# Moving row sums and norm matmuls behind the value matmuls, and summing a layer's last tile in halves

## The chip, the core and the metric

One core of a Trainium2 chip runs the whole program. The metric is the device time of one launch in microseconds (us), the median of several runs. Engines are named as the profile names them: PE (TensorE matmul) with its weight loads PEld, DVE (VectorE), ACT (ScalarE), POOL (GpSimd), SP (SyncE, which here only issues DMAs).

## The reference

The input x has 2048 rows of 1024 values. Two layers run one after the other, each an attention block and a spectral block:

```python
x = x + attention(layernorm(x))   # 32 heads of 32 columns, 2048 queries by 2048 keys, then @ wo
x = x + spectral(layernorm(x))    # rfft2, times complex weights, irfft2
...
scores = einsum("bhqd,bhkd->bhqk", q, k) * 32 ** -0.5
p = softmax(scores); o = einsum("bhqk,bhkd->bhqd", p, v); return o @ wo
```

## The kernel before, in words

**The main loop of attention.** The 32 heads are taken in 8 groups g of 4 heads, the queries in 4 chunks c of 512, the keys in 16 tiles kt of 128. One pass of the loop, here called a step, is one (g, c, kt). In each step `S` writes scores into two tiles of the PSUM pool `psS` (three tiles of two banks each), and ACT takes the exponential of both into two `p` tiles (line 552; the `p` pool has eight tiles, so four steps). K and Q are split into two fp16 parts, so `S` is 12 matmuls on 32 rows each. In every even step `PV` multiplies the `p` tiles of the two steps before by V (line 558): four fp32 matmuls per step, each on 32 columns of the array, which the trace shows as 16 PE instructions for the two steps.

**Row sums.** The softmax's denominators are summed on DVE: `add` adds each `p` tile into an accumulator `acc` of two halves (line 569 for the first two steps of a chunk together, which overwrites `acc`; line 571 after that). There is one `acc` only. When a chunk is through, `fin` multiplies `acc` by ones on PE (`z`, line 577, four fp32 matmuls on 32 columns, eight PE instructions in the trace, into a tile of `psS`), and DVE transposes, inverts, transposes back and scales the chunk's output (lines 578 to 584). `out` then makes two fp16 parts of it, the high one on ACT (line 590), the low one on POOL (line 591), and a DMA stores them.

**Work between the steps.** In odd steps a generator `fill` feeds PE with the projections of the groups to come, paced by `slots`: 8 or so matmuls at a time of `qk_chunk` (K or Q, line 328, 24 matmuls into a PSUM tile `x`) or of `v_tiles` (line 372). Tile `x` is a pool of one. At the end of a `qk_chunk`, `split` reads it twice: ACT writes the high fp16 part (line 167), DVE the low one (line 168), and only then can the next projection start. POOL squares the high part (`sq`, line 332). After the last of four chunks of a K or a Q the phase is put into `left_norms`, and `norms` turns the squares into norms: four bf16 matmuls on 32 columns (line 345) into a tile of `psS`, a maximum on DVE (line 347), and after a Q a bias by way of POOL (`partition_all_reduce`, lines 353 to 358). Group 7 has no projections left; there the slots carry the products with `wo` (`wo_part`, and `wo_rest` for tiles that are ready).

**Order.** In the main loop PE and ACT keep the order in which the source issues their work (`manual_schedule`). The queues of DVE, POOL and SP are ordered by a planner, which works ahead of the run and fixes each queue once.

**A layer's end.** The last four row tiles t = 0 to 3 wait for the last chunk's output. `first(t, ds)` does the products with `wo` for the groups ds of 0 to 6, `last(t)` the one for group 7, by `wo_last`: DVE adds the residual `xres` over all 1024 columns (line 460), takes `bn_stats` of both halves (line 462), a DMA stores the tile, DVE folds it (lines 146, 147), POOL works out scale and bias in eight small instructions (`scale_bias`, lines 119 to 124, 489, 490), ACT and DVE apply them (lines 685, 686). `xres` has a pool of two tiles (`wqk`), so tile t needs tile t-2 to be stored and folded first. `fold_rests` does the same for the twelve tiles before. The spectral block's first transposes (line 762) need all sixteen tiles. In this part only PE keeps the source's order. At the end of the program `combine_flags` gathers checks over all partitions (`partition_all_reduce`, line 1108, on POOL).

The lines of the main loop that are changed, in short:

```python
if kt % 2 == 0:
    for w in pend: PV(*w)          # the two steps before
    late, pend = pend, []
for w in late[:1]:
    add(*w)                        # kt 14 of the last chunk at kt 0, kt 15 at kt 1
    if w[2] == NKT - 1: fin(*w[:2]); done = [w[:2]]
late = late[1:]
if kt == 5 and done: out(*done.pop())
```

and `slots` runs `while left_norms: norms()` ahead of each odd step's projection matmuls.

Of the kernel before, what the change touches and what calls it, by code (L numbers as in the profile page):

```python
# [6 lines left out]
F32 = mybir.dt.float32  # L7
# [4 lines left out]
AF = mybir.ActivationFunctionType  # L12
ALU = mybir.AluOpType
# [88 lines left out]
SW = 2.0 ** 8  # L102
SQ = 2.0 ** 5
SO = 2.0 ** 5
# [23 lines left out]
def ln_stats(nc, sm, cst, st, mv):  # L128

    nc.vector.bn_aggr(mv, st)  # L130
    return ln_scale(nc, sm, cst, mv, nc.vector)
# [9 lines left out]
def fold(nc, x, out, a, eng=None):  # L141

    xv = x.rearrange("p (a u g q) -> p g a u q", a=8, g=2, q=8)[:, :, a]
    ov = out.rearrange("p (u g a q) -> p g a u q", g=2, a=8, q=8)[:, :, a]
    eng = eng or nc.gpsimd
    eng.tensor_tensor(ov[:, 0], xv[:, 0], xv[:, 1], op=ALU.add)
    eng.tensor_tensor(ov[:, 1], xv[:, 0], xv[:, 1], op=ALU.subtract)
# [23 lines left out]
def run(g):  # L171
    for _ in g:
        pass
# [93 lines left out]
def attention(nc, tc, layer, ap, xin, yd, wts, wo, cst, dram, flags):  # L267
# [6 lines left out]
    sq, on, on2, sm = ap.sq, ap.on, ap.on2, ap.sm  # L274
    psS = psum("at_psS", 3, space=PSUM)
# [13 lines left out]
    V, K, Q, bias, nrm, mx = {}, {}, {}, {}, {}, {}  # L289
# [47 lines left out]
    left_norms = []  # L337

    def norms():
        kind, g = ph = left_norms.pop(0)  # L340
        if g not in mx:
            mx[g] = sm.tile([128, 2], F32, name="mqk")
        ps = psS.tile([128, 2, 512], F32, name="s")
        for c in range(4):
            nc.tensor.matmul(ps[32 * c:32 * c + 32, 0], cst["bones"], nrm[ph][:, c], start=True, stop=True)
        i = 0 if kind == "k" else 1
        nc.vector.reduce_max(mx[g][:, i:i + 1], ps[:, 0], axis=AX.X)
        if kind == "q":
            mkbias(g)
# [75 lines left out]
    def wo_mm(p, c, t, n, ds, start=True, stop=True):  # L425

        for d in ds:
            oh, ol = ((olast[c][:, i] if d == 7 else osb[c][:, i, d])[:, t * 128:t * 128 + 128] for i in range(2))
            wh, wl = (wo_t[i][d // 4][:, d % 4, n * 512:n * 512 + 512] for i in range(2))
            for i, (a, b) in enumerate(((oh, wh), (oh, wl), (ol, wh))):  # L430
                nc.tensor.matmul(p, a, b, start=start and d == ds[0] and i == 0, stop=stop and d == ds[-1] and i == 2)  # L431
                yield

    def xres(c, t):
        x = wqp.tile([128, 1024], F32, name="xres", tag="wqk")
        r0 = c * 512 + t * 128
        nc.sync.dma_start(x, xin[r0:r0 + 128, :])
        return x
# [80 lines left out]
    for c in range(NCH):  # L519
        t = 4 * c + 4  # L520
# [33 lines left out]
    def PV(g, c, kt):  # L554
        if kt == 0:
            O[g, c] = psO.tile([128, 512], F32, name="o")
        for h in range(4):
            nc.tensor.matmul(O[g, c][32 * h:32 * h + 32], V[g][:, kt, 32 * h:32 * h + 32], P[g, c, kt, h // 2][:, h % 2],  # L558
                             start=kt == 0, stop=kt == NKT - 1)
        if kt == NKT - 1:  # L560
            o = ap.oc.tile([128, 512], F32, name="oc")
            nc.scalar.copy(o, O[g, c])
            O[g, c] = o
# [9 lines left out]
    def fin(g, c):  # L573
        zt = on.tile([128, 16, 32], F32, name="zt")
        z = psS.tile([128, 2, 512], F32, name="s")[:, 0]
        for h in range(4):
            nc.tensor.matmul(z[32 * h:32 * h + 32], cst["ones"], acc[h // 2][:, h % 2], start=True, stop=True)  # L577
        nc.vector.transpose(zt.rearrange("p a b -> p (a b)"), z)
        rc = sm.tile([128, 16], F32, name="rc")
        nc.vector.reciprocal(rc, zt[:, :, 0])  # L580
        nc.vector.tensor_max(flags["r"], flags["r"], rc)
        r = on.tile([128, 512], F32, name="zt")
        nc.vector.transpose(r.rearrange("p (a b) -> p a b", b=32), rc.unsqueeze(2).broadcast_to([128, 16, 32]))
        nc.vector.scalar_tensor_tensor(r, O[g, c], SO, r, op0=ALU.mult, op1=ALU.mult)
        O[g, c] = r
# [8 lines left out]
        else:  # L594
            olast[c] = t

    pend, done, late = [], [], []
    fill, lwo, wof = filler(), load_wo(), wo_parts()
    left, parts, rests = 16, 20, list(range(12))

    def slots(f, sums, n, steps):

        while sums:
            k = max(1, int(n / sums + 0.5))
            m = -(-steps // k)
            for i in range(0, steps, m):
                while left_norms:
                    norms()
                for _ in range(min(m, steps - i)):
                    next(f, None)  # L610
                n -= 1
                yield sums - (i + m >= steps)
            sums -= 1

    with tc.manual_schedule(engines={mybir.EngineType.PE, mybir.EngineType.Activation}):
        for g in range(NG):
            todo = sum(sums(ph) for ph in beside.get(g, []))
            sl = slots(fill, todo, 22 if g == NG - 2 else 32, 24)
            wsl = slots(wof, 4, 10, 21)
            for u in range(NCH * NKT):  # L620
                c, kt = divmod(u, NKT)
                S(g, c, kt)
                if kt % 2 == 0:
                    for w in pend:
                        PV(*w)
                    late = pend
                    pend = []
                for w in late[:1]:
                    add(*w)
                    if w[2] == NKT - 1:  # L630
                        fin(*w[:2])
                        done = [w[:2]]
                late = late[1:]
                if kt == 5 and done:
                    out(*done.pop())
                pend.append((g, c, kt))
                if kt % 2 == 0:
                    continue
                if todo:
                    todo = next(sl)  # L640
                elif g == NG - 2:
                    if left:
                        run(lwo)
                        left = 0
                    if next(wsl, None) is not None and u == NCH * NKT - 1:
                        run(wsl)
                elif g == NG - 1:
                    t = rests[0] if rests else 16
                    if (t // 4 < c - 1 or t // 4 == c - 1 and kt >= 7) and (kt % 4 == 3 or not parts):
                        wo_rest(rests.pop(0))  # L650
                    elif parts:
                        parts -= 1
                        for _ in range(21):
                            next(wof)
                if g == NG - 2 and todo < 4:
                    for _ in range(2):
                        if left > (8 if todo == 3 else 0):
                            next(lwo, None)
                            left -= 1
        for w in pend:  # L660
            PV(*w)
        for w in late + pend:
            add(*w)
        run(wof)
        for t in rests:
            wo_rest(t)
    with tc.manual_schedule(engines={mybir.EngineType.PE}):
        ps, xs, folds = [], [], fold_rests()

        def first(t, ds):  # L670
            if ds[0] == 0:
                ps.append(psS.tile([128, 2, 512], F32, name="s"))
                xs.append(xres(3, t))
            for n in range(2):
                run(wo_mm(ps[t][:, n], 3, t, n, ds, start=ds[0] == 0, stop=False))

        def last(t):
            o = ap.x[:, 12 + t]
            st = wo_last(3, t, ps[t], xs[t], xs[t], False)
            mv = sm.tile([128, 2], F32, name="mv")  # L680
            nc.vector.bn_aggr(mv, st)
            r, b = scale_bias(mv, 1, 2.0)
            fold(nc, xs[t], o, slice(0, 8), nc.vector)
            ov = o.rearrange("p (u g q) -> p g u q", g=2, q=64)
            nc.scalar.activation(ov[:, 0], ov[:, 0], AF.Identity, bias=b, scale=r)
            nc.vector.tensor_scalar(ov[:, 1], ov[:, 1], r, None, op0=ALU.mult)

        def some(n):
            for _ in range(n):
                next(folds, None)  # L690
        first(0, range(7))
        fin(NG - 1, NCH - 1)
        out(NG - 1, NCH - 1, nc.vector)
        some(6)
        first(1, range(7))
        last(0)
        some(4)
        first(2, range(7))
        last(1)
        run(folds)  # L700
        first(3, range(4))
        last(2)
        first(3, range(4, 7))
        last(3)
    psum.close()
    small.close()

# [491 lines left out]
```

## Time and profile before

| | us |
|---|---|
| median of 3 runs | 3951.18 (3951.08 to 3956.0) |
| the profiled execution | 3952.66, span 3950.8 |
| PE busy | 3770.9 (95%) |
| DVE busy | 3225.5 (82%) |
| ACT busy | 2893.9 (73%) |
| POOL busy | 643.4 (16%) |
| granted TensorE clock | 0.985 |

The span is what lies between the first and the last instruction; some 2 us of the execution lie around it. The main loop of layer 0 runs from about 128 to 1655 us of the span, that of layer 1 from about 2107 to 3614; the rest is preparation, the layers' ends and the spectral blocks. A row of the timeline gives start, length, engine, line, what it writes and reads, how many instructions were merged, and in brackets the idle time before it and what ended it.

### The profile page before, as it was taken

The numbers are of one execution on the slowest core, as the hardware profiler recorded it, in microseconds if no ns is written. First come the engines' busy times: TensorE is split into PE (matmuls) and PEld (weight loads), VectorE is DVE, ScalarE is ACT, GpSimd is POOL, SyncE is SP. The second block draws the span as 40 slices with busy tenths as digits, with TensorE's granted clock in tenths as the row PEclk, the third lists the DMA queues.
The fourth block names the chain that finished last, engine by engine and source line by source line (L and its number), as shares of the span: only waits on it lengthen the run. The fifth ranks groups of instructions, "written<-read, shape, count | busy, mean of one in ns | idle before, by whom it ended". The sixth has DMA issues, their size and how long they took to land.

```text
span 3950.8 us, 80100 instructions
## 1 busy us (share of the span) xinstructions
PE 3770.9 (95%) x33204; PEld 1671.8 (42%) x33204; DVE 3225.5 (82%) x3845; ACT 2893.9 (73%) x3565; POOL 643.4 (16%) x591
## 2 busy tenths in 40 slices
PE   7999999999999999989989999999999999999898
PEld 5322432342243233378854334333422432333787
DVE  6699888989998978866765998899899888788456
ACT  4587887888788766658745888888888887665585
POOL 1011011101110200014321220122021111000143
PEclk9999999999999999999999999999999999999999
DMA  3000000000000211143120000000000002122323
GB/s 116 14 15 19 12 12 17 17 14 19 12 23 12 89 52 68 54 177 108 55 86 12 15 23 12 12 17 24 8 17 17 17 12 89 57 73 83 120 94 102
DMA packets 97559, 177.31 MB, mean 45 GB/s; under 512 B 7200, under 2 KB 52896, under 8 KB 96160
## 3 DMA queue, kind: packets, MB, share of 16 engines
q1 hardware_dynamic: 97040, 172.03, 12.7%
q8 instruction: 262, 4.29, 0.4%
q14 instruction: 113, 0.93, 0.1%
q10 hardware_dynamic: 144, 0.07, 0.0%
HBM read 123.83 MB, written 48.23 MB: 44 GB/s over the span
## 4 chain that ended last, share of the span: by engine, by line
PE 76%; DVE 9%; issue 7%; ACT 4%; POOL 3%; DMA 1%; SPq 0%; DVEq 0%; ACTq 0%; POOLq 0%
PE o L558 21%; PE s L548 17%; PE x L328 13%; PE x L372 8%; PE x L431 6%; DVE R L571 2%; ACT p L552 2%; PE ps L833 2%; PE ps L771 2%; PE s L577 1%; PE o L372 1%; PE ps L762 1%; PE ps L948 1%; PE o L328 1%; PE ps L902 1%
## 5 line engine op out<-in xcount | busy, mean ns | idle before, releaser
L552 ACT ACTIVATE p<-s,bias 128x1024 f32<-128x1024 f32 x2048 | 2168.3, 1111 | 585.0 <-PE s L548 573.8
L571 DVE TENSOR_TENSOR R<-R,p 128x1024 f32<-128x1024 f32 x1792 | 2145.8, 1250 | 142.2 <-ACT p L552 138.1
L558 PE MATMUL o<-p,R 128*32 128x512 f32 x8192 | 985.0, 598 | 0.0
L328 PE MATMUL x<-big,wqk 128*128 128x512 f16 x2880 | 686.6, 384 | 22.7 <-DVE R L168 8.2
L548 PEld LDWEIGHTS <-R 32*128 32x128 f16 x12288 | 231.1, 92 | 781.1 <-issue 664.8
L328 PEld LDWEIGHTS <-wqk 128*128 128x128 f16 x3072 | 277.6, 98 | 460.7 <-issue 169.4
L548 PE MATMUL s<-R 32*128 32x512 f16 x6144 | 431.9, 379 | 19.0 <-ACT p L552 15.5
L548 PE MATMUL s<-Q,R 32*128 32x512 f16 x6144 | 432.0, 378 | 11.9 <-ACT p L552 10.6
L558 PEld LDWEIGHTS o<-p,R 128*32 128x32 f32 x8192 | 213.7, 109 | 523.5 <-issue 522.9
L591 POOL TENSOR_TENSOR ohl<-zt,ohl 128x512 f16<-128x512 f32 x62 | 180.0, 2903 | 1473.4 <-ACT ohl L590 1473.4
L372 PEld LDWEIGHTS <-big 128*128 128x128 f16 x3072 | 293.3, 99 | 117.2 <-issue 69.8
L372 PE MATMUL x<-wv,big 128*128 128x256 f16 x2688 | 323.5, 277 | 12.5 <-DVE R L168 6.0
L569 DVE SCALAR_TENSOR_TENSOR R<-p 128x1024 f32<-128x1024 f32 x128 | 153.8, 1203 | 197.5 <-ACT p L552 197.1
L332 POOL TENSOR_TENSOR sq<-R 128x512 bf16<-128x512 f16 x96 | 142.4, 1483 | 703.0 <-ACT R L167 702.5
L431 PE MATMUL x<-big 128*128 128x512 f16 x1008 | 228.0, 380 | 0.0
L431 PEld LDWEIGHTS <-big 128*128 128x128 f16 x1344 | 126.8, 98 | 177.9 <-issue 35.8
L881 DVE TENSOR_TENSOR H<-G,H 128x512 f16<-128x512 f32 (+1 forms) x68 | 46.8, 688 | 106.1 <-ACT H L880 105.9
L833 PE MATMUL ps<-cbi,H 128*128 128x256 f16 (+1 forms) x792 | 99.1, 273 | 6.2 <-ACT H L880 4.3
L826 ACT COPY U<-ps 64x256 f32<-64x256 f32 (+1 forms) x272 | 97.0, 357 | 7.9 <-PE ps L833 2.7
L826 ACT COPY B<-ps 64x256 f32<-64x256 f32 (+1 forms) x272 | 97.0, 356 | 6.7 <-PE ps L833 2.4
L332 POOL TENSOR_TENSOR sq<-Q 128x512 bf16<-128x512 f16 x32 | 45.1, 1409 | 321.3 <-ACT Q L167 321.3
L833 PE MATMUL ps<-cb,big 128*128 128x256 f16 x780 | 96.3, 273 | 0.0
(418 smaller groups left out, 3145.0 us busy)
## 6 DMA issues: line engine op xcount, KB each, us to landing
wst<-in_wp SPq DMA_DIRECT2D x96, 256.0 KB, 3.0
R<-y SPq DMA_DIRECT2D x32, 512.0 KB, 5.2
w<-in_w SPq DMA_DIRECT2D x60, 256.0 KB, 2.6
od<-ohl SPq DMA_DIRECT2D x56, 256.0 KB, 2.4
big<-od SPq DMA_DIRECT2D x16, 896.0 KB, 7.1
y<-R SPq DMA_DIRECT2D x20, 512.0 KB, 2.6
R<-in_x SPq DMA_DIRECT2D x16, 512.0 KB, 6.6
wst<-in_wo SPq DMA_DIRECT2D x32, 256.0 KB, 3.0
```

The lines of the kernel that those rows point to most:

```text
L328: nc.tensor.matmul(ps, a, b, start=d == 0 and i == 0, stop=d == 7 and i == 2)
L332: nc.gpsimd.tensor_tensor(nrm[ph][:, c], t[:, 0], t[:, 0], op=ALU.mult)
L372: nc.tensor.matmul(ps[:, j], l, r, start=d == 0 and i == 0, stop=d == 7 and i == 2)
L431: nc.tensor.matmul(p, a, b, start=start and d == ds[0] and i == 0, stop=stop and d == ds[-1] and i == 2)
L548: nc.tensor.matmul(s[h // 2][:, h % 2], K[g][r, a, kt * 128:kt * 128 + 128], Q[g][r, b, c * 512:c * 512 + 512], start=i == 0, stop=i == 2)
L552: nc.scalar.activation(p, s[hf], AF.Exp, bias=bias[g], scale=SCALE / (SQ * SQ))
L558: nc.tensor.matmul(O[g, c][32 * h:32 * h + 32], V[g][:, kt, 32 * h:32 * h + 32], P[g, c, kt, h // 2][:, h % 2], start=kt == 0, stop=kt == ...
L569: nc.vector.scalar_tensor_tensor(acc[hf], P[g, c, 0, hf], 1e-34, p, op0=ALU.add, op1=ALU.add)
L571: nc.vector.tensor_add(acc[hf], acc[hf], p)
L591: eng.tensor_tensor(t[:, 1], r, t[:, 0], op=ALU.subtract)
L826: nc.scalar.copy(ov[64 * r:64 * r + 64, a0:a0 + m, x], tl[64 * x:64 * x + 64, :m, r])
L833: nc.tensor.matmul(out, l, r, start=k == 0, stop=k == len(mm_) - 1)
```

## The change

1. In the main loop `fin` moves from step 1 of the next chunk, right behind the scores, to step 2, behind the eight value matmuls that step issues. `add` for the last key tile stays at step 1 and only notes the chunk in `ends`.
2. `norms` leaves `slots` and stands behind the value matmuls of every even step.
3. At a layer's end POOL, too, keeps the source's order.
4. The products for tile 2 start before `last(0)` (three groups), and tile 3 isn't prepared ahead: a new function `whole(3)` does all its products at the very end, in two halves of 512 columns; while PE works on the second, DVE adds the residual of the first, takes its statistics, stores it and folds it. Scale and bias are worked out on DVE but for one power on POOL.

```diff
-    pend, done, late = [], [], []
+    pend, ends, done, late = [], [], [], []
...
-                while left_norms:
-                    norms()
                 for _ in range(min(m, steps - i)):
                     next(f, None)
...
                 if kt % 2 == 0:
                     for w in pend:
                         PV(*w)
+                    if ends and kt == 2:
+                        fin(*ends[0])
+                        done = [ends.pop()]
+                    while left_norms:
+                        norms()
                     late = pend
                     pend = []
                 for w in late[:1]:
                     add(*w)
                     if w[2] == NKT - 1:
-                        fin(*w[:2])
-                        done = [w[:2]]
+                        ends = [w[:2]]
...
-    with tc.manual_schedule(engines={mybir.EngineType.PE}):
+    with tc.manual_schedule(engines={mybir.EngineType.PE, mybir.EngineType.Pool}):
...
+        def whole(t):
+
+            p, x, o = psS.tile([128, 2, 512], F32, name="s"), xres(3, t), ap.x[:, 12 + t]
+            st = sm.tile([128, 2, 6], F32, name="st")
+            r0 = 3 * 512 + t * 128
+            for n in range(2):
+                sl = slice(n * 512, n * 512 + 512)
+                run(wo_mm(p[:, n], 3, t, n, range(8)))
+                nc.vector.scalar_tensor_tensor(x[:, sl], p[:, n], 1.0 / (SO * SW), x[:, sl], op0=ALU.mult, op1=ALU.add)
+                nc.vector.bn_stats(st[:, n], x[:, sl])
+                nc.sync.dma_start(yd[r0:r0 + 128, sl], x[:, sl])
+                fold(nc, x, o, slice(4 * n, 4 * n + 4), nc.vector)
+            mv = sm.tile([128, 2], F32, name="mv")
+            r = ln_stats(nc, sm, cst, st, mv)
+            b = sm.tile([128, 1], F32, name="b1")
+            nc.vector.scalar_tensor_tensor(b, mv[:, 0:1], -2.0, r, op0=ALU.mult, op1=ALU.mult)
+            ov = o.rearrange("p (u g q) -> p g u q", g=2, q=64)
+            nc.scalar.activation(ov[:, 0], ov[:, 0], AF.Identity, bias=b, scale=r)
+            nc.vector.tensor_scalar(ov[:, 1], ov[:, 1], r, None, op0=ALU.mult)
+
         first(0, range(7))
         fin(NG - 1, NCH - 1)
         out(NG - 1, NCH - 1, nc.vector)
         some(6)
         first(1, range(7))
+        first(2, range(3))
         last(0)
         some(4)
-        first(2, range(7))
+        first(2, range(3, 7))
         last(1)
         run(folds)
-        first(3, range(4))
         last(2)
-        first(3, range(4, 7))
-        last(3)
+        whole(3)
```

## The prediction

> **What bounds the kernel now.** I read the page first, then the timeline at the start of a chunk, the busy time by windows, the views of single lines (who waits for whom), and the timeline of the layers' ends.
>
> ```profile
> PE 3770.9 (95%) x33204; PEld 1671.8 (42%) x33204; DVE 3225.5 (82%) x3845; ACT 2893.9 (73%) x3565; POOL 643.4 (16%) x591
> L552 ACT ACTIVATE p<-s,bias 128x1024 f32<-128x1024 f32 x2048 | 2168.3, 1111 | 585.0 <-PE s L548 573.8
> L571 DVE TENSOR_TENSOR R<-R,p 128x1024 f32<-128x1024 f32 x1792 | 2145.8, 1250 | 142.2 <-ACT p L552 138.1
> ```
>
> PE leads: ACT idles 574 us for scores. But DVE isn't far behind, and this change touches just its place. The chunk that starts at 2514.60 shows the pattern:
>
> ```profile
> 2514.60 0.83 PE L548 MATMUL s<-R 32*128 32x512 f16 x12
> 2515.35 1.92 PE L558 MATMUL o<-p,R 128*32 128x512 f32 x16
> 2517.21 0.82 PE L548 MATMUL s<-R 32*128 32x512 f16 x12
> 2517.97 1.06 PE L577 MATMUL s<-R,ones 128*32 128x512 f32 x8
> 2518.07 2.12 ACT L552 ACTIVATE p<-s,bias 128x1024 f32<-128x1024 f32 x2
> 2518.96 1.90 PE L328 MATMUL x<-big,wqk 128*128 128x512 f16 x8
> 2519.22 1.23 DVE L569 SCALAR_TENSOR_TENSOR R<-p 128x1024 f32<-128x1024 f32 x1 [2.12 <-ACT p L552]
> 2520.80 0.83 PE L548 MATMUL s<-R 32*128 32x512 f16 x12
> 2523.41 0.82 PE L548 MATMUL s<-R 32*128 32x512 f16 x12
> 2524.38 5.76 DVE L571 TENSOR_TENSOR R<-R,p 128x1024 f32<-128x1024 f32 x5
> 2526.00 0.82 PE L548 MATMUL s<-R 32*128 32x512 f16 x12
> ...
> 2514.60:2559.90 45.30, 44.27 (x405) 13.30 (x407) 42.52 (x42) 36.71 (x38) 9.26 (x4) 1.00 0.02 8
> ```
>
> Steps start at 2514.60, 2517.21, 2520.80, 2523.41, 2526.00. A plain step is 2.60 of PE; step 1 with the row sums is 3.59. DVE adds at 5.76 / 5 = 1.15 per half, 2.30 per step. The last row (windows: PE, PEld, DVE, ACT, POOL busy) leaves DVE 45.30 - 42.52 = 2.78 us idle in the chunk, and 2.12 of these are the wait ahead of line 569. There is hardly any slack elsewhere.
>
> **The change, part by part.**
>
> *Fewer changes of kind on PE.* Sixteen value matmuls take 2517.21 - 2515.35 = 1.86, the eight of the row sum, alone between scores and projection, 2518.96 - 2517.97 = 0.99. Eight more of the same kind therefore cost 0.87, and 0.12 is the price of standing alone. The row sums join the value matmuls 62 times (31 per layer): -7.4. The norms do 28 times (14 per layer); no row shows their bf16 passes behind fp32 ones, so 0 to 0.12 each, and I take 0.12, as the shape on the array is the same: -3.4. Together -11.
>
> *Waits at the row sums.* The waits of the row sums for the last adds go, as DVE has over 4 us more (first row; the others serve below):
>
> ```profile
>   DVE R L571: 6.1, 7
> ...
>   POOL sq L332: 7.0, 5
> ...
>   DVE R L168: 8.2, 8
>   DVE Q L168: 6.3, 3
> ...
>   PE s L548: 4.6, 7
> ```
>
> (idle time of line 577 ended by the adds; of the norm matmuls by POOL; of the projections by DVE's split, two rows; of scores held by the norms' maximum.) -6.
>
> *The accumulator is free later.* There is one `acc`, and line 569 overwrites it, so it waits for the row sum to have read it. Now it starts 2519.22 - 2517.21 = 2.0 after step 1 began, held by ACT alone. Then: step 1 without sums 2.60, scores and value matmuls 0.75 + 1.74, the sum's first half 0.44, and some 0.2 until DVE knows: 5.7. DVE starts each chunk 3.7 us later, 62 times, with nothing to put into the pause but a split (0.6). This doesn't lengthen the chunk at once: `p` holds four steps, and up to about 5 us of lateness at a chunk's end cost nothing, as the next pause absorbs them. But DVE is late throughout. Line 569 starts 3.1 after step 2; from it to the first line 571 lie 5.16 now, some 4.6 if the split goes into the pause; so the adds of step 2 end 3.1 + 4.6 + 2.3 = 10.0 after that step began, where exponentials (0.86 + 2.12) and one add (1.2) would allow 4.2: late by 5.8. PE gives back 0.30 per step, and 0.87 more at step 2, which the sum makes longer: 5.8 - 5 x 0.30 - 0.87 = 3.4 left at step 7. A POOL operation that gets in between costs DVE more: two adds take 3.56 then, 2.35 without.
>
> ```profile
> 2710.26 9.17 DVE L571 TENSOR_TENSOR R<-R,p 128x1024 f32<-128x1024 f32 x8
> 2719.94 3.56 DVE L571 TENSOR_TENSOR R<-R,p 128x1024 f32<-128x1024 f32 x2
> 2724.03 2.35 DVE L571 TENSOR_TENSOR R<-R,p 128x1024 f32<-128x1024 f32 x2
> ...
> 2712.37 8.07 POOL L591 TENSOR_TENSOR ohl<-zt,ohl 128x512 f16<-128x512 f32 x1 [9.16 <-ACT ohl L590]
> ...
>   L591 POOL TENSOR_TENSOR ohl<-zt,ohl x62: 1162/1831/9315, 193.0 to 3583.7; 128x512 f16<-128x512 f32 x62
> ...
> 2722.47 0.38 PE L345 MATMUL s<-sq,bones 128*32 128x512 bf16 x1 [2.16 <-POOL sq L332]
> ```
>
> So about 4.6 late at step 7. What is behind DVE's queue there? The split that frees tile `x` for the next projection. Layer 0 shows its price, where DVE is late by its own extra work:
>
> ```profile
> 606.24 7.74 DVE L571 TENSOR_TENSOR R<-R,p 128x1024 f32<-128x1024 f32 x6
> 606.53 0.83 PE L548 MATMUL s<-R 32*128 32x512 f16 x12
> 611.73 0.82 PE L548 MATMUL s<-R 32*128 32x512 f16 x12
> 613.90 0.68 DVE L168 SCALAR_TENSOR_TENSOR Q<-x,Q 128x512 f16<-128x512 f32 x1
> 614.64 4.21 PE L328 MATMUL x<-big,wqk 128*128 128x512 f16 x12 [2.08 <-DVE Q L168]
> ```
>
> Step 7 starts at 606.53; its adds end at 613.98, late by 3.2; the split stands behind them in the queue, and the projection of step 9, due at 611.73 + 0.76, waits 2.1. The rule from this row: wait = lateness - 1.1. At 4.6 that is 3.5 per chunk if the queue keeps this order; each half add that the planner puts behind the split takes off 1.15. In the source the split stands before the adds of its own step, and the planner, too, sees the pause; yet the row shows a queue that doesn't follow what really is late. Between 0 (four halves overtaken) and 3.5 (none) I take 1.6, one or two of them. Chunks with K or Q projections: all four of groups 0, 2, 4, three of group 6, the first two of groups 1, 3, 5: 21 per layer, 42. 42 x 1.6 = +67; the waits that stand there now and are part of it (8.2 + 6.3 + 4.6 = 19) come off: +48. V projections free `x` by ACT alone, and group 7 has DVE time to spare: 0 there.
>
> *Norms and POOL.* The norm in the second chunk of groups 0 to 6 (14 times) follows the last square by less: it stands one set of scores earlier (0.76). The square queues behind `out`'s low half, which takes 1.8 us mostly but 8.07 where eight adds follow without a gap. DVE that never pauses makes this the rule. Now these waits are 7.0 in all; then 0 to 3 each, and I take 1.0, nearer to today's rows: 14 - 7 = +7. ACT's copy for `out` at step 5 isn't late: the row sum's DVE work ends some 8 us after step 2, step 5's exponentials later.
>
> In a sentence that the sum doesn't use: the Trainium skill, "SBUF — State Buffer", section "SBUF: two separate sides", says that a VectorE instruction with two SBUF inputs and a GpSimd one share a port pair as an exclusive lock, held for the whole instruction. Taken literally GpSimd would wait for one add at most (1.2 + 1.8 = 3.0 us); the row's 8.07 over eight adds speaks against so early a turn, and by the rule this term would be -7 and the total 3961.
>
> *The layers' ends.*
>
> ```profile
> 1679.78 0.61 PE L431 MATMUL s<-big,ohl 128*128 128x512 f16 x2 [2.59 <-ACT ohl L590]
> 1680.82 1.89 PE L431 MATMUL s<-big,ohl 128*128 128x512 f16 x4 [0.43 <-DVE ohl L591]
> 1704.04 1.46 PE L431 MATMUL s<-big,ohl 128*128 128x512 f16 x6
> 1715.72 2.01 PE L762 MATMUL ps<-ident,R 128*128 128x128 f32 x8 [10.23 <-ACT R L685]
> ...
> 1708.53 1.23 DVE L460 SCALAR_TENSOR_TENSOR xres<-s,xres 128x1024 f32<-128x1024 f32 x1 [2.00 <-DMA xres<-in_x]
> ...
> 3681.03 2.01 PE L762 MATMUL ps<-ident,R 128*128 128x128 f32 x8 [16.26 <-ACT R L685]
> ...
> 3658.60 0.40 POOL L1108 PARTITION_ALL_REDUCE fa<-f  x1 [6.90 <-issue]
> 3667.13 0.25 POOL L119 TENSOR_SCALAR v<-mv 128x1 f32<-128x1 f32 x1 [8.13 <-issue]
> ```
>
> Tile 2's first groups fill the waits of 2.59 + 0.43. From line 460 to the transposes lie 7.2 us; in halves, with 0.6 each, and one POOL step instead of eight, about 4.5. But `xres` of tile 3 comes by a DMA that follows tile 1's store; it ends the wait today. So between 0 and -7 for layer 0; I take -4. Layer 1 idles 6.0 longer, since the planner put the checks' all-reduce among the tiles (6.90 + 8.13 of POOL time); with POOL in source order it comes later, where the spectral block's first stage leaves POOL idle. -4 - 6 = -10, at worst +5, if its wait then holds DVE. SP's queue gets one store more per layer: 0, hidden behind the constants' loads. Together -14.
>
> **The sum.** -11 - 6 + 48 + 7 - 14 = +24. The profiled execution is 3952.7 (span 3950.8 and 1.9 around it), 1.5 above the median 3951.2; so 3977 for a like execution, 3975 as the median.
>
> **Rivals.**
>
> *Faster: the planner re-sorts DVE's queue.* It sees the pause before the row sum, sets splits and maxima ahead of the late adds, and PE never waits. Then -11 - 6 - 19 - 7 - 14 = -57, 3894; with a few waits left, 3906. It decides below (11 + 6 + 19 - 7 + 14) / 42 = 1.0 us of wait per chunk. For it: the source order; against it: the layer-0 rows.
>
> *Much slower: the queue stays as it is.* 2.8 per chunk instead of 1.6, norms at 1.5: +24 + 50 + 7 = +81, 4032; with 3.5, 4062.
>
> *The all-reduce stays among the tiles* although POOL keeps source order, because it lies outside the ordered part: layer 1 gains 4, not 10: 3981. This goes with any other case.
>
> **How the numbers follow.** About 8 us (0.2%) is what a measurement tells from no change. Queue re-sorted, 3894 to 3943: 0.36. Gains and waits even out, within 8: 0.12. Forecast, 3959 to 4010: 0.32 (that is its own range). Much slower, to 4062: 0.20. Range 3903 to 4040, which leaves out some 0.07 below and 0.11 above. Faster 0.36, same 0.12, slower 0.52.
>
> **What would show it.** In the profile after: step 1 shorter by 0.99 and step 2 longer by 0.87; line 569's idle time ended by PE line 577 and not by ACT, some 5 us each; line 328 waiting for DVE line 168 by 50 to 80 us in all (14.5 now); `out` on POOL with a median well above 1.83; line 345 waiting more for POOL; line 762 after 6 to 8 us of idle time in both layers, the all-reduce behind it. Wrong, if line 328's wait stays near 15: then the queue was re-sorted.

## The result, and the profile after

The changed kernel takes 4178.5 us (median of 4 runs, 4173.8 to 4186.1); the kernel before, on the same chip, 3953.6 (3951.1 to 3960.1). The ratio is 1.0569 (95% interval 1.0556 to 1.0582): 5.7% slower. The forecast was 3975, the range 3903 to 4040; the direction came out, which the forecast had given a chance of 0.52, and the size did not. The profiled execution took 4186.1 with a span of 4184.3.

First the page of the changed kernel (per engine: busy time, share of the span, instructions; per group: busy time, mean ns | idle time before it and what ended most of it):

```profile
PE 3826.3 (91%) x33204; PEld 1698.1 (41%) x33204; DVE 3242.1 (77%) x3863; ACT 2895.1 (69%) x3565; POOL 540.7 (13%) x577
L328 PE MATMUL x<-big,wqk 128*128 128x512 f16 x2880 | 734.3, 403 | 157.4 <-DVE R L168 112.3
L569 DVE SCALAR_TENSOR_TENSOR R<-p 128x1024 f32<-128x1024 f32 x128 | 153.9, 1204 | 285.2 <-PE s L577 249.1
```

The row of line 328 in the kernel before:

```profile
L328 PE MATMUL x<-big,wqk 128*128 128x512 f16 x2880 | 686.6, 384 | 22.7 <-DVE R L168 8.2
```

The number of PE instructions is as before, yet PE is busy 55 us longer (3826.3 against 3770.9), and its share of the span falls. Line 569 is now held by the row sums, line 328 by the split. The waits of the changed kernel (who waited for whom: us, times, longest) complete this:

```profile
DVE R L569 <- PE s L577: 249.1, 62, 8.8
PE x L328 <- DVE R L168: 112.3, 29, 4.8
PE x L328 <- DVE Q L168: 36.8, 7, 6.7
PE x L372 <- DVE R L168: 32.5, 6, 5.9
```

Projections wait 112.3 + 36.8 + 32.5 = 181.6 us for the split, 42 times. Where the span grew can be read from the timelines' starts (us between the first score matmul, the last row sum, and the spectral block's first transpose of each layer; "PE idle" is the sum of its matmuls' idle times in the two main loops):

| | main loop, layer 0 | layer 1 | PE idle in both | end, layer 0 | layer 1 |
|---|---|---|---|---|---|
| before | 1538.9 | 1519.0 | 68.5 | 48.8 | 54.8 |
| after | 1644.9 | 1633.3 | 233.1 | 56.1 | 60.9 |

So the main loops cost +220.3, of which 164.6 are idle time of PE and the other 55.7 slower work; the ends cost +13.4; the rest of the program is unchanged (-0.2).

One chunk shows both parts of the main loop's loss. It is the third chunk of group 2 in layer 1, in the timeline of the changed kernel, PE and DVE:

```profile
2716.28 0.83 PE L548 MATMUL s<-R 32*128 32x512 f16 x12
2717.03 2.76 PE L328 MATMUL x<-big,wqk 128*128 128x512 f16 x12
...
2722.23 1.04 PE L577 MATMUL s<-R,ones 128*32 128x512 f32 x8
2723.30 1.22 DVE L569 SCALAR_TENSOR_TENSOR R<-p 128x1024 f32<-128x1024 f32 x1 [2.15 <-PE s L577]
...
2729.83 1.29 DVE L168 SCALAR_TENSOR_TENSOR wqk<-wst,wqk 128x512 f16<-128x512 f32 x2
2731.03 13.25 DVE L571 TENSOR_TENSOR R<-R,p 128x1024 f32<-128x1024 f32 x10
2733.61 0.83 PE L548 MATMUL s<-R 32*128 32x512 f16 x12
...
2744.21 0.68 DVE L168 SCALAR_TENSOR_TENSOR Q<-x,Q 128x512 f16<-128x512 f32 x1
2744.93 4.84 PE L328 MATMUL x<-big,wqk 128*128 128x512 f16 x12 [5.30 <-DVE Q L168]
```

Step 1 starts at 2716.28 and line 569 at 2723.30, 7.0 later; it was 2.0 before. (The third chunk of each group from 0 to 6 has so long a step 1; in the others that follow a row sum it is 6.0 to 6.5, and in group 7 it is 9.0.) Ten half adds (13.25 us) then stand in DVE's queue ahead of the split of line 168. Step 7 starts at 2733.61, its adds end at 2744.28. The projection of step 9 waits 5.30 us for the split. And then its 12 matmuls take 4.84 us, where the same 12 take 2.76 in the second row. The windows of the same timeline (length, then PE, PEld, DVE, ACT, POOL busy, then the granted clock PEclk) say why:

```profile
2716.28:2719.73 3.45, 3.45 (x28) 1.31 (x25) 0.00 (x0) 2.96 (x4) 0.00 (x0) 1.00 0.02 5
2738.81:2749.71 10.90, 5.60 (x28) 1.87 (x25) 10.61 (x10) 2.49 (x3) 0.00 (x0) 0.69 0.00 0
```

In the step without a wait the granted clock is 1.00, in the stretch of the wait and the projection behind it 0.69 (0.56 over the projection alone). The Trainium skill, "TensorE: Matmul & The Clock Gate", section "What's actually happening", says that the array falls to half its clock after an idle window of about 3.4 us and needs about as long of work to come back. The rows agree in kind: 12 matmuls at half the clock would take twice 2.76, 5.5 us as an estimate from the row, and 4.84 were measured. But here shorter waits were enough at times. In the kernel before, 12 projections took 4.21 at a granted clock of 0.63 behind a wait of 2.08 (a row of the prediction), and full speed behind one of 2.07:

```profile
985.25 2.75 PE L328 MATMUL x<-big,wqk 128*128 128x512 f16 x12 [2.07 <-DVE Q L168]
```

The ends of the layers, in the timeline (layer 0, then, behind the dots, layer 1):

```profile
1815.83 0.69 DVE L701 SCALAR_TENSOR_TENSOR xres<-s,xres 128x512 f32<-128x512 f32 x1 [3.00 <-DMA xres<-in_x]
1816.57 6.75 PE L431 MATMUL s<-big 128*128 128x512 f16 x21 [15.18 <-DVE xres L701]
1824.01 0.69 DVE L701 SCALAR_TENSOR_TENSOR xres<-s,xres 128x512 f32<-128x512 f32 x1 [4.61 <-PE s L431]
1829.11 2.01 PE L783 MATMUL ps<-ident,R 128*128 128x128 f32 x8 [5.14 <-ACT R L710]
...
3874.16 0.40 POOL L1129 PARTITION_ALL_REDUCE fa<-f  x1 [19.03 <-DVE f L1125]
3886.31 0.25 POOL L119 TENSOR_SCALAR v<-mv 128x1 f32<-128x1 f32 x1 [11.75 <-issue]
3903.13 6.25 PE L431 MATMUL s<-big 128*128 128x512 f16 x21 [20.45 <-DVE xres L701]
```

The transposes wait only 5.1 us now, in both layers, as they were meant to. But the matmuls of the second half wait 15.2 and 20.5 us until DVE has read the first half, and DVE waits for the load of the residual. Behind that wait 21 matmuls take 6.75 and 6.25 us, where 21 of the same line take 4.70 earlier in the same end (at 1796.05). The all-reduce still stands among the tiles.

### The profile page after: what moved, and what is told of

Read it like the earlier page. It is cut to its first block, busy times and chain, and to the rows that moved or that the text cites. A ratio compares the mean times of both kernels' runs of the same rounds, so it can differ in the third digit from the quotient of the medians.

```text
span 4184.3 us, 79879 instructions
## 1 busy us (share of the span) xinstructions
PE 3826.3 (91%) x33204; PEld 1698.1 (41%) x33204; DVE 3242.1 (77%) x3863; ACT 2895.1 (69%) x3565; POOL 540.7 (13%) x577
## 4 chain that ended last, share of the span: by engine, by line
PE 67%; DVE 15%; issue 11%; ACT 2%; DMA 2%; POOL 2%; SPq 0%; DVEq 0%; POOLq 0%; ACTq 0%
PE o L558 18%; PE s L548 14%; PE x L328 13%; PE x L372 7%; DVE R L571 5%; PE x L431 5%; DVE R L569 2%; PE ps L792 1%; PE ps L854 1%; PE s L577 1%; ACT p L552 1%; PE o L372 1%; PE ps L783 1%; PE ps L969 1%; PE o L328 1%
## 5 line engine op out<-in xcount | busy, mean ns | idle before, releaser
L571 DVE TENSOR_TENSOR R<-R,p 128x1024 f32<-128x1024 f32 x1792 | 2181.3, 1267 | 123.3 <-ACT p L552 122.7
L328 PE MATMUL x<-big,wqk 128*128 128x512 f16 x2880 | 734.3, 403 | 157.4 <-DVE R L168 112.3
L328 PEld LDWEIGHTS <-wqk 128*128 128x128 f16 x3072 | 289.5, 101 | 614.2 <-issue 345.3
L569 DVE SCALAR_TENSOR_TENSOR R<-p 128x1024 f32<-128x1024 f32 x128 | 153.9, 1204 | 285.2 <-PE s L577 249.1
L372 PE MATMUL x<-wv,big 128*128 128x256 f16 x2688 | 329.7, 280 | 38.9 <-DVE R L168 32.5
L591 POOL TENSOR_TENSOR ohl<-zt,ohl 128x512 f16<-128x512 f32 x62 | 85.0, 1371 | 1533.6 <-ACT ohl L590 1533.6
L168 DVE SCALAR_TENSOR_TENSOR R<-x,R 128x512 f16<-128x512 f32 x88 | 60.1, 683 | 80.3 <-ACT R L167 80.3
L431 PE MATMUL s<-big 128*128 128x512 f16 x336 | 77.8, 392 | 35.6 <-DVE xres L701 35.6
```

The costliest lines, as they stand in the source:

```text
L328: nc.tensor.matmul(ps, a, b, start=d == 0 and i == 0, stop=d == 7 and i == 2)
L372: nc.tensor.matmul(ps[:, j], l, r, start=d == 0 and i == 0, stop=d == 7 and i == 2)
L569: nc.vector.scalar_tensor_tensor(acc[hf], P[g, c, 0, hf], 1e-34, p, op0=ALU.add, op1=ALU.add)
L571: nc.vector.tensor_add(acc[hf], acc[hf], p)
L591: eng.tensor_tensor(t[:, 1], r, t[:, 0], op=ALU.subtract)
```

## The experiments

Theory A: the accumulator comes free late; the planner leaves the split behind the half adds, which then are late; PE waits, and runs at a reduced clock after the wait. Rivals: the norms behind the value matmuls, POOL's new order, or DVE having no time left whatever the order.

### One part of the change at a time

`e1_fin_only` is the kernel before with this edit alone:

```diff
                     for w in pend: PV(*w)
+                    if ends and kt == 2:
+                        fin(*ends[0]); done = [ends.pop()]
...
                     if w[2] == NKT - 1:
-                        fin(*w[:2]); done = [w[:2]]
+                        ends = [w[:2]]
```

> The kernel before with one part of the change: the row sums move to step 2 behind the value matmuls; norms and layers' ends stay. Theory A (the accumulator comes free late, DVE is late through the chunk, the split stands behind its adds, and PE waits and then runs slowly): this part is the whole loss of the main loop, +220 us by the two traces (106 in layer 0, 114 in layer 1), the ends as before: 4174, between 4160 and 4190. Theory B (the norms behind the value matmuls share in the loss, since POOL's squares come late): at least 50 less, below 4125. Theory C (the ends with POOL in source order hurt beyond their 13 us): the main loop still +220, so the same 4174.

Measured: 4174.8, ratio 1.0556 (1.0538 to 1.0574). From its page:

```profile
L328 PE MATMUL x<-big,wqk 128*128 128x512 f16 x2880 | 730.5, 402 | 158.1 <-DVE R L168 113.3
```

The row is that of the changed kernel within 4 us, and line 569 idles 243.0 us for the row sums (249.1 there); the main loops take 1639.5 and 1632.4. This one edit alone lengthens the main loops by 214.0 of the changed kernel's 220.3: it is the loss of the main loops but for 6 us.

`e2_ends_only` is the kernel before with the new layers' ends (`whole`, the order of the products, POOL in source order).

> The kernel before with the layers' ends alone changed (the order of the products, the last tile in halves, POOL in source order). Theory A: only what the traces show between the last row sum and the first spectral transpose, +7.3 and +6.1: 3967, between 3961 and 3973. Theory C (POOL's order reaches back into the main loop through the planner): above 3985. My prediction's figure for this part was -14: 3940.

Measured: 3966.0, ratio 1.0023 (1.0014 to 1.0033). Main loops 1541.0 and 1519.2, ends 56.0 and 57.3. POOL's order doesn't reach back into the main loop.

`e3_fin_back` is the changed kernel with `fin` again in step 1 right behind `add`:

```diff
-                    if ends and kt == 2:
-                        fin(*ends[0])
-                        done = [ends.pop()]
...
-                        ends = [w[:2]]
+                        fin(*w[:2])
+                        done = [w[:2]]
```

> The changed kernel with the row sums put back to step 1; norms stay behind the value matmuls and the ends stay new. Theory A: main loop as before, less 3 to 6 for fewer changes of kind at the norms, ends +13: 3962, between 3956 and 3970. Theory B: the norms cost by themselves, above 3985.

Measured: 3970.8, ratio 1.0034 (1.0020 to 1.0048), just above what was expected. Against `e2_ends_only`, from which it differs by the norms alone, the main loops are -0.2 and +5.3: no gain by the norms can be seen.

### What turns a late accumulator into a wait

`e5_dve_order` is the changed kernel, row sums late as they are, with one more engine in source order:

```diff
-    with tc.manual_schedule(engines={mybir.EngineType.PE, mybir.EngineType.Activation}):
+    with tc.manual_schedule(engines={mybir.EngineType.PE, mybir.EngineType.Activation, mybir.EngineType.DVE}):
```

> The changed kernel, but DVE too keeps the source's order in the main loop, so that each split stands ahead of the adds of its own and the next step, whose exponentials come later. The accumulator is as late as in the changed kernel. Theory A1 (the wait is a matter of queue order: four half adds stand ahead of the split): waits of line 328 for line 168 fall from 112 to under 20 us, the slow projections behind them go, main loop -200: 3965 with the ends' +13, between 3945 and 3990. Theory A2 (DVE has no time left: it idles 4.6 us per chunk where it had 2.8 us in all, and PE must wait for it somewhere whatever the order): (4.6 - 2.8) x 42 = 76 at least remain: above 4040. If source order holds DVE behind the row sum's transposes or behind a split that waits for a load, line 552 or 571 would show it, and the time could be above 4178.

Measured: 3948.1, ratio 0.9980 (0.9970 to 0.9990): 230 us faster than the changed kernel, and a little faster than the kernel before in spite of the slower ends. Its page:

```profile
L328 PE MATMUL x<-big,wqk 128*128 128x512 f16 x2880 | 684.3, 383 | 14.8 <-DVE Q L168 7.3
```

and its timeline in group 2, layer 1, at the start of the first chunk:

```profile
2467.39 0.83 PE L548 MATMUL s<-R 32*128 32x512 f16 x12
2469.98 0.83 PE L548 MATMUL s<-R 32*128 32x512 f16 x12
2473.45 0.83 PE L548 MATMUL s<-R 32*128 32x512 f16 x12
...
2476.13 2.35 DVE L569 SCALAR_TENSOR_TENSOR R<-p 128x1024 f32<-128x1024 f32 x2
2478.40 4.62 DVE L571 TENSOR_TENSOR R<-R,p 128x1024 f32<-128x1024 f32 x4
2482.94 0.68 DVE L168 SCALAR_TENSOR_TENSOR R<-x,R 128x512 f16<-128x512 f32 x1
2483.86 0.39 PE L548 MATMUL s<-R 32*128 32x512 f16 x4
```

Line 569 starts 2476.13 - 2467.39 = 8.7 us after step 1 began, later than in the same chunk of the changed kernel (2623.33 - 2617.11 = 6.2). But only four half adds of line 571 stand between it and the split, which is done about when step 7 begins. DVE has time enough; the rival that it has none falls. The order decides. Main loops: 1526.8 and 1506.6, 24.5 less than before. Source order changes all of DVE's queue, so that this run shows the order as the cause, not the split's place alone.

`e8_before_order` has the same edit on the kernel before.

> The kernel before with one edit: DVE keeps the source's order in the main loop. With the row sums at step 2, source order made the main loop 24.5 us shorter than that of the kernel before (1526.8 + 1506.6 against 1538.9 + 1519.0). This run parts the two causes. If source order does it alone (waits for splits and maxima, 19 us in the kernel before): 3935, between 3930 and 3941. If fewer changes of kind and the row sums' waits for adds do it (11 + 6 of my sum): only some 7 us here, 3950, between 3944 and 3957. If at step 1 source order makes DVE wait for the row sums' transposes: above 3957.

Measured: 4087.3, ratio 1.0335 (1.0315 to 1.0355): none of the two expected causes, but the case that was named last and without a size. In the waits (who waited for whom: us, times, longest):

```profile
DVE zt L578 <- PE s L577: 119.7, 62, 3.6
PE s L577 <- DVE R L571: 65.8, 34, 3.5
```

With the sums in step 1, PE waits 34 times for the last adds (line 577; the row sums themselves take 122.7 us of PE's time, 74.1 in the kernel before), and DVE, which in source order may not go ahead, stands idle in every chunk until the row sum is there (line 578). Neither half of the pair pays alone: source order alone costs 132 us and late row sums alone 218, each against the kernel before on the same chip; both together gain in the main loop.

`e6_two_acc` gives each second chunk an accumulator of its own, and takes the room from the exponentials (`pp` six tiles instead of eight):

```diff
+    acc2 = acp.tile([128, 2, 2, 512], F32, name="acc2")
+    accs = [ap.acc, [acc2[:, 0], acc2[:, 1]]]
...
+        acc = accs[c % 2]          # in add and in fin
```

> The changed kernel with two accumulators that chunks use in turn; to make room the pool of exponentials has six tiles instead of eight (three steps instead of four). Row sums stay at step 2, DVE's queue is the planner's. Theory A (the wait of the first adds for the row sum is the start of it all): line 569 no longer waits for line 577, DVE is on time, line 328's waits for line 168 fall from 112 to under 25 us and the slow projections go: main loop some 220 less than in the changed kernel, 3960 with the ends' +10, up to 3990 if three steps of exponentials hold ACT back. Rival (the row sum's transposes and the scaling on DVE, which now fall into step 2 to 4, make DVE late by themselves): the waits stay above 60 us, time above 4060.

Measured: 3978.4, ratio 1.0062 (1.0042 to 1.0081). Its page (the edit moves lines 328, 569 to 329, 573; the second accumulator's group of line 573 waits for ACT alone as well):

```profile
L329 PE MATMUL x<-big,wqk 128*128 128x512 f16 x2880 | 689.5, 385 | 36.6 <-DVE R L168 18.6
L573 DVE SCALAR_TENSOR_TENSOR R<-p 128x1024 f32<-128x1024 f32 x64 | 75.5, 1221 | 118.9 <-ACT p L555 118.9
```

With the wait for the row sum gone, the split's waits and the slow matmuls go too (36.6 us of idle time ahead of the line and 385 ns for a matmul, 157.4 and 403 in the changed kernel), with DVE's queue still the planner's. The row sum's own work on DVE isn't the cause. The main loops stay 22.5 above the kernel before; whether three steps of exponentials cost that was not tried by itself.

`e13_sums_first` puts `fin` ahead of the value matmuls of step 2, so that the accumulator is late by 1.86 us less:

```diff
+                    if ends and kt == 2: ...
                     for w in pend: PV(*w)
-                    if ends and kt == 2: ...
```

> The changed kernel with the row sums at step 2 ahead of the value matmuls instead of behind them: the accumulator is free 1.86 us earlier, 3.1 us later than in the kernel before instead of 5.0. Theory A (a wait is the lateness less a constant, and the slow matmuls behind it come on top): each of the 48 long waits 1.9 us shorter, -91, and a part of the 56 us of slow matmuls: 4070, between 4045 and 4090. Rival (any lateness beyond DVE's slack costs the whole stall): above 4130.

Measured: 4078.7, ratio 1.0296 (1.0279 to 1.0312). In the timeline of group 2, layer 1, the four chunks' long waits go from 4.81, 3.68, 5.30 and 3.02 us to 3.09, 1.68, 3.58 and 1.87: -1.7, -2.0, -1.7, -1.2, close to one for one. The long stall isn't all or nothing.

### The slow matmuls

`e7_filler` puts useless matmuls where PE would wait:

```diff
+    FILL = {(0, 7): 18, (1, 9): 14, (2, 9): 20, (3, 7): 11}
...
+            d = psS.tile([128, 2, 512], F32, name="s")
+            for _ in range(FILL[c, kt] + 4 * (g % 2 and c == 1)):
+                nc.tensor.matmul(d[:, 0], xh[0][:, 0, 0:128], xh[0][:, 0], start=True, stop=True)
```

> The changed kernel with useless matmuls (128x512 fp16, 11 to 20 of them, 2.4 to 4.4 us) put into PE's queue just ahead of the projections that wait longest for the split: steps 7 and 9 of the chunks with K or Q projections. Nothing of the work is removed; the wait for the split ends when it did. Theory K (after a wait of 3 to 7 us PE's clock is reduced, and the projections behind it run slowly; 12 of them take 4.84 where 2.76 is usual): the projections behind the filler take 2.8 to 3.2, PE's work falls by the 55 us that the changed kernel's lies above the kernel before, less what the remaining gap of about 1 us costs: 4135, between 4120 and 4150. Rival (they are slow because DVE and POOL catch up at the same time and disturb their reads, or because the records are stretched): no gain, 4170 or more.

Measured: 4242.0, ratio 1.0725 (1.0706 to 1.0744), 63 slower than the changed kernel. As a whole the expectation failed, but for a reason that the timeline shows beside the effect that was looked for. The first chunk of group 2, layer 1, and then the second:

```profile
2676.48 4.04 PE L621 MATMUL s<-big 128*128 128x512 f16 x18
2681.27 1.89 PE L328 MATMUL x<-big,wqk 128*128 128x512 f16 x8 [0.74 <-DVE R L168]
...
2735.98 4.94 PE L621 MATMUL s<-big 128*128 128x512 f16 x14 [6.55 <-DVE mqk L347]
```

In the first chunk the filler (line 621) takes the place of the wait, and 8 projections take 1.89. In the changed kernel, at the same step:

```profile
2639.22 3.57 PE L328 MATMUL x<-big,wqk 128*128 128x512 f16 x8 [4.81 <-DVE R L168]
```

3.57 for the same 8. The chunk is 2.0 us shorter with useless work in it. In the windows of that stretch the clock, which lies at 0.66 in the changed kernel (first row), is full (second row, of the run with fillers):

```profile
2633.58:2642.72 9.14, 4.33 (x25) 1.31 (x22) 9.14 (x9) 2.92 (x3) 1.63 (x1) 0.66 0.09 30
```

```profile
2675.64:2683.09 7.45, 6.69 (x43) 2.75 (x40) 7.45 (x7) 2.91 (x3) 1.63 (x1) 1.00 0.12 37
```

DVE is busy throughout in both, POOL as long in both: contention isn't the cause, the idle time is. In the second chunk the filler's own PSUM tile was still held by the norms' maximum (line 347), 102.0 us over 14 times, and this lost more than the fillers gained. `e12_filler_less` leaves that position out (`FILL` without `(1, 9)`).

> The changed kernel with the useless matmuls only at step 7 of first and last chunks and step 9 of third chunks, not at step 9 of second chunks, where their PSUM tile itself had to wait 6.5 us for the norms' maximum in the run with all of them. Theory K (the clock is reduced after the wait): as in that run's chunks, -2.0 for each first chunk (12), -2.1 for each third (6), -2.7 for each last (6): -53 altogether, 4125, between 4115 and 4140. Rival (no clock effect): 4170 or more.

Measured: 4150.4, ratio 1.0491 (1.0475 to 1.0507): 28 us less than the changed kernel (34 less if each is taken against the kernel before on its own chip), by adding work, but not 53. In layer 1 the main loop is 27.3 shorter, as expected; in layer 0 only 9.0. There the fourth chunks of groups 0, 2 and 4 have a second late split, and with fillers these chunks are 2.6 to 3.4 us longer. The projection of step 13, group 2, in the changed kernel, and then with fillers, behind a row of DVE:

```profile
720.58 4.23 PE L328 MATMUL x<-big,wqk 128*128 128x512 f16 x12 [2.47 <-DVE R L168]
```

```profile
706.34 0.69 DVE L257 TENSOR_REDUCE wm<-wst 128x1 f32<-128x512 f32 x1 [2.78 <-DMA wst<-in_wp]
...
718.59 5.24 PE L328 MATMUL x<-big,wqk 128*128 128x512 f16 x12 [5.05 <-DVE R L168]
```

What PE gained at step 7, DVE lost again: it now comes to the check of a weight tile (line 257, ahead of the adds in its queue) before the tile is loaded, and waits 2.8 us in each of the three chunks. The next split comes later still, and the 12 projections behind it take 5.24 instead of 4.23.

### The layers' ends, and the better version

`e9_two_tiles` is `e2_ends_only` with a PSUM tile for each half:

```diff
-            p, x, o = psS.tile([128, 2, 512], F32, name="s"), xres(3, t), ap.x[:, 12 + t]
+            x, o = xres(3, t), ap.x[:, 12 + t]
...
-                run(wo_mm(p[:, n], 3, t, n, range(8)))
+                p = psS.tile([128, 2, 512], F32, name="s")[:, 0]
+                run(wo_mm(p, 3, t, n, range(8)))
```

> The kernel before with the new layers' ends, but each half of the last tile has a PSUM tile of its own. Theory T (in the changed kernel the second half's matmuls wait 15.2 and 20.5 us for DVE to have read the first half, only because both are one tile, and DVE itself waits for the residual's load): that wait goes, the second half's adds follow the first's at once, and the part from the last row sum to the first transpose falls from 56.0 and 57.3 to about 48 and 50: 3951, between 3945 and 3957. Rival (the load of the residual sets the end and the second half's sums are as late as before): 3966 as without this edit.

Measured: 3953.9, ratio 0.9994 (0.9985 to 1.0004). Its timeline at the end of layer 0:

```profile
1704.50 0.81 PE L431 MATMUL s<-big,ohl 128*128 128x512 f16 x3
1715.17 1.29 DVE L700 SCALAR_TENSOR_TENSOR xres<-s,xres 128x512 f32<-128x512 f32 x2 [2.96 <-DMA xres<-in_x]
1722.00 2.01 PE L782 MATMUL ps<-ident,R 128*128 128x128 f32 x8 [16.69 <-ACT R L709]
```

PE is through with both halves at 1705, and DVE takes both at once when the residual has come. The ends fall to 50.2 and 50.7 (from 56.0 and 57.3). In layer 0 that is still no better than before, since the load of the residual sets the end as it did then.

`e11_order_ends` and `e14_order_two_tiles` are the changed kernel with DVE in source order and two tiles; the first also loads the residuals early, into tiles of the exponentials' pool:

```diff
+        for t in range(4):
+            x = pp.tile([128, 1024], F32, name="xn", tag="p")
+            nc.sync.dma_start(x, xin[3 * 512 + t * 128:3 * 512 + t * 128 + 128, :])
+            xs.append(x)
```

> The changed kernel with DVE in source order in the main loop, a PSUM tile for each half of the last tile, and the four residual tiles loaded early into tiles of the exponentials' pool, so that no load waits for a store. Main loop as in the run with DVE in source order, -24.5 against the kernel before; ends at 43 and 45 instead of 48.8 and 54.8, set by PE's matmuls and one short tail: 3915, between 3906 and 3928. If the residual's load did not bind once the halves are apart: as the next run.

> The same without the early loads of the residual. Main loop -24.5, ends about 50 and 52 to 57: 3931, between 3922 and 3940; slower than the run with early loads by 10 to 20, if the residual's load is what the last tile waits for.

Measured: 3931.4, ratio 0.9928 (0.9915 to 0.9942), and 3935.1, ratio 0.9947 (0.9932 to 0.9962). Both beat the kernel before and the changed one. The ends are 52.2 and 47.8 with early loads, 50.8 and 58.1 without: the load no longer binds, but in layer 0 of `e11_order_ends` the planner sets checks of the next weights (line 780, which in `e14_order_two_tiles` all come behind the last tile) among the last tiles' steps on DVE. PE waits for a PSUM tile that DVE reads too late, and the last tile's second half (line 705) waits its turn as well:

```profile
1691.24 1.27 DVE L780 TENSOR_REDUCE wom<-wo 128x1 f32<-128x512 f32 x2
1693.96 4.69 PE L431 MATMUL s<-big 128*128 128x512 f16 x21 [3.43 <-DVE xn L460]
...
1705.39 1.26 DVE L780 TENSOR_REDUCE wom<-wo 128x1 f32<-128x512 f32 x2
1707.24 0.68 DVE L705 SCALAR_TENSOR_TENSOR xn<-s,xn 128x512 f32<-128x512 f32 x1
```

The expected 43 and 45 didn't come. The end of layer 1, which has no such checks, is 10.3 shorter with early loads, yet the two profiled spans differ by 0.4 and the two intervals overlap: that the early loads gain as a whole isn't shown.

## Why the prediction was wrong in size

By the terms of its sum, which made +24:

- *Late accumulator, +48: this is the step that failed.* It measured +220 (164.6 idle, 55.7 slow): the projections' waits for the split are 181.6 in the 42 of the changed kernel, 4.3 each for the 1.6 that I took. The mechanism, its place and the rule from the layer-0 row held: in the chunk shown, the adds of step 7 end 2744.28 - 2733.61 - 4.3 = 6.4 late, and 6.4 - 1.1 is the 5.3 of the wait. Three sizes were off. (1) Of the four half adds ahead of the split I let the planner set one or two behind it, and took 1.6 of a possible 3.5; it set none behind. This was the choice without a row, against the only row at hand. (2) The lateness was 6.4 in this chunk and not 4.6. Line 569 came 7.0 after step 1 and not 5.7: step 1 of this third chunk carries 12 projections (2.76) instead of 8, and in every chunk line 569 starts when the whole row sum is through, not its first half (1.07 after line 577 began, not 0.64); in the other chunks with projections that makes 6.0 to 6.5. Then two weight splits (1.29) stood in DVE's queue, and ten half adds took 13.25 where 11.5 are usual, since two operations of POOL got in between (see below), so that the lateness didn't melt by 0.30 per step. (3) I had no term for the matmuls behind a wait. The row was in my own fence: 12 projections in 4.21 behind 2.08 of idle time, where they take 2.76. I read its bracket and not its length. Spread over 42 waits the 55.7 are 1.3 us each.
- *Waits instead of an absorbed pause.* "Up to about 5 us of lateness cost nothing" holds for the exponentials' pool: ACT waits for an add of line 571 for 1.3 us in all, before and after. It says nothing of what else is queued on the late engine.
- *Fewer changes of kind, -11.* The row sums' part is right: in the run with DVE in order, steps 1 and 2 take 2.59 and 3.47, as the -0.99 and +0.87 said. The norms' part isn't seen.
- *The row sums' waits, -6: read too high.* In the changed kernel line 577 waits for no add any more. But of the 6.1 us in the row of the prediction 5.1 are idle time of the weight loads (PEld), while PE still had work; PE itself waited 1.0 us, once. With DVE in order the weight loads wait 4.3 again, and PE not at all.
- *Norms and POOL, +7: wrong in sign for the whole change.* The norms' waits for the squares fell from 7.0 to 1.2, and `out` on POOL became shorter, 1.37 on average after 2.90 (view of line 591 in the changed kernel, with the shortest, median and longest in ns, and the rows of `out` and DVE in the chunk shown above):

```profile
L591 POOL TENSOR_TENSOR ohl<-zt,ohl x62: 1183/1288/2061, 191.9 to 3809.4; 128x512 f16<-128x512 f32 x62
...
2732.02 1.25 POOL L591 TENSOR_TENSOR ohl<-zt,ohl 128x512 f16<-128x512 f32 x1 [10.47 <-ACT ohl L590]
2732.17 2.19 DVE L571 TENSOR_TENSOR R<-R,p 128x1024 f32<-128x1024 f32 x1
```

  DVE doesn't pause there: it adds without a gap through all 62 of them. `out` gets in behind the add under way, and it is the next add that takes 2.19 instead of 1.22; a square does the same to another of the ten adds (2.06). Why POOL is let in so soon here, and not in the kernel before, isn't shown. In `e3_fin_back`, where the norms are moved and the sums aren't, `out` is as before (2.90) and the norms wait 10.4 for the squares: there the sign was right.

- *The layers' ends, -14: +13.4.* The short tail was right (7.2 to about 5 between the last add and the transposes). What I didn't see is that one PSUM tile for both halves makes the second half's matmuls wait for DVE's read of the first, which itself waits for the residual, the very load that I had quoted as ending the old wait. The layer-1 part fell by the rival that I priced at 6: the all-reduce stays among the tiles, outside the ordered part, and POOL's next operation comes 11.75 us after it.

Of the signs that I had named, line 569 behind line 577 (249.1 us over 62 chunks, 4.0 each, for 5) and the idle time ahead of the transposes (5.1 for 6 to 8) came out; line 328's wait for the split was 149 for 50 to 80; `out` and the norms' wait went the other way, and the all-reduce didn't move.

The rival "the queue stays as it is" was the right one, and its 4062 too low by the slow matmuls and by lateness. The rival "faster" has its core in the run with DVE in source order: the gain that it priced at -57 with the ends is there at -24.5 in the main loop, but it takes the queue's order to get it, which the change left to the planner.

## What to carry to other kernels

When a step that frees a buffer is moved later, look up the next writer's engine and list everything in that engine's queue until it has caught up; the wait is paid by whoever needs an unrelated result behind it. A queue that a planner fixed ahead of the run doesn't re-sort itself for a delay: either give the late engine the source's order together with the move, or don't move (each alone lost over 130 us here, the pair gained). And price a PE wait of several us with the slower matmuls behind it (here 1.4 to 2.5 us more behind waits of 4.8 us and longer); a row that has a length and a bracket says both.

## What the runs showed of the hardware that I had not expected

- After PE waits of 4.8 and 5.3 us the granted clock over the stretch was 0.66 and 0.69, and 8 and 12 projections took 3.57 and 4.84 instead of 1.89 and 2.76. All 24 waits of 4.8 us and more in the changed kernel's main loops were followed by projections at a granted clock of 0.50 to 0.65. Behind shorter waits both cases stand in the same trace: 8 projections behind 3.68 us of wait took 3.57 at one place and 1.89 at another. Useless matmuls in the wait (18 in 4.04 us) kept the clock at 1.00, and the kernel got 28 us faster by them.
- A GpSimd operation on SBUF beside back-to-back adds on DVE was let in at once or kept out for long. With DVE in source order, `out` on POOL took up to 30.3 us, and 6.4 on average; in the changed kernel, with DVE adding through every one of them, never more than 2.1. The view of line 591 with DVE in source order:

```profile
L591 POOL TENSOR_TENSOR ohl<-zt,ohl x62: 1152/1834/30258, 191.5 to 3567.4; 128x512 f16<-128x512 f32 x62
```

  Here it cost nothing to wait, since nothing waits for `out`; to be let in cost DVE 1.0 us for one add. The rule that the prediction weighed (the Trainium skill, "SBUF — State Buffer", section "SBUF: two separate sides") would let it in after the add under way, some 3.0 us at most by the prediction's working. The changed kernel agrees with that, the 30.3 us don't; what decides between the two stays open.
